# Five weight loads of an MM-DiT attention block issued as two transfers each

## The chip, the cores and the metric

The kernel runs on one core of one Trainium2 chip. The metric is the device time of one execution in microseconds (us). The time before is the median of three executions. Two numbers are kept apart: the device time, and the span of a profiled execution, which runs from the first instruction that the profiler records to the last one.

## The reference

Two streams of tokens, image (2 x 256 tokens) and text (2 x 32), share one attention. D is 1152, all tensors are bf16, and there is one head of width D.

```python
mod_i = (_silu(c) @ wmod_img).reshape(B, 6, 1, D)      # the same for _txt
shi, sci, gai = mod_i[:, 0], mod_i[:, 1], mod_i[:, 2]
hi = _layernorm(x_img) * (1 + sci) + shi               # ht from x_txt
qkvi = hi @ wqkv_img                                   # qkvt = ht @ wqkv_txt
q = concat([qt, qi]); k = concat([kt, ki]); v = concat([vt, vi])
p = softmax(einsum('bqd,bkd->bqk', q, k) * D ** (-0.5))
a = einsum('bqk,bkd->bqd', p, v)
out_i = x_img + gai * (a[:, Nt:] @ wo_img)
out_t = x_txt + gat * (a[:, :Nt] @ wo_txt)
```

Of the six modulation blocks of each `wmod` only the first three are read. So the core reads fourteen weight blocks of 1152 x 1152 (2592 KB each), seven per stream: shift, scale, gate, q, k, v and output.

## The kernel before

The contraction dimension is cut into KT = 9 rows of 128 partitions. A weight block lies in SBUF as a tile of 128 partitions x 9 x 1152, and every matmul that contracts over D runs a loop `kt` from 0 to 8 over that tile.

**Loads.** All weight loads go through the queue of SyncE (SP). The helper `load_w` (L73 to L77) takes one of the five buffers of the pool `w`, or a buffer that another tensor has left (argument `home`), and issues one `dma_start` at L76 for each pair in `ksplits`. `K3` cuts a block into three transfers of three rows (864 KB each), and `K2`, which is defined and used by no call, into one of five rows (1440 KB) and one of four (1152 KB). Without `ksplits` a block is one transfer of nine rows.

The loads that the change touches stand together at L443 to L453, in the order in which SP issues them: `w_k_i` (three parts), `w_sh_t`, `w_sc_t`, the text tokens `x_t` (144 KB), `w_q_t`, `w_k_t`, `w_ga_i`, `w_v_t` (three parts), `w_o_i`, `w_ga_t`, `w_o_t` (three parts). A load whose buffer is still being read waits on SP for the reader, and everything behind it on SP waits too.

**Who reads them.** The order of work is written out by hand (`manual_schedule`). TensorE runs, in this order: the image products (v at L255, q and k at L514); inside the k product the strips of the text modulation (`w_sh_t`, `w_sc_t` at L400 and L404) and the text q (`w_q_t`, L580); then the text k (`w_k_t`, L580); the scores with the image gate (`w_ga_i`, L630, L635 and L651); the text v (`w_v_t`, L688); the attention output (L753); the output projection of the image (`w_o_i`, L845), in its midst the text gate (`w_ga_t`, L818) and the text projection (`w_o_t`, L863); and the last chunks of the image. GpSimd (POOL) reads `w_o_i` once more at L829, to fold the gate into the last columns of the last chunk.

**Stores.** Image tiles 0 to 2 are stored whole at L856 from SP. The text output leaves in four pieces at L877, one from SP and three from ScalarE (ACT). The last image tile leaves in four pieces at L854: 384 and 384 columns from SP, 256 from ACT, and the last 128 from SP.

**Semaphores.** The framework gives each transfer that SP or ACT issues one of eight semaphores, in turn, called here H0 to H7. SP and ACT share the eight. Before a transfer is issued, its queue waits until the transfer eight places earlier, which had the same semaphore, has landed (where that is not yet known from an earlier wait). There are 51 such transfers, numbered here 0 to 50: 45 from SP and 6 from ACT. Number 50, the last store, thus has H2. The two stores before it, numbers 48 and 49, have H0 and H1. POOL's transfers have eight semaphores of their own.

**The end.** When the kernel's body is done (the profile gives this code the line L918), SP runs nine semaphore instructions: the first waits for two of POOL's semaphores, and the other eight for H0, H1, and so on to H7, each together with one semaphore of another engine or of POOL's queue. Then it drains, and two barriers over all engines follow.

Of the kernel before, what the change touches and what calls it, by code (L numbers as in the profile page):

```python
# [14 lines left out]
def kernel(  # L15
# [19 lines left out]
    B, NI, D = x_img.shape  # L35
# [34 lines left out]
    def w_view(src):  # L70
        return src.rearrange("(kt p) n -> p kt n", p=P)

    def load_w(src, c0, ksplits=((0, KT),), home=None):  # L73
        t = wpool.tile([P, KT, D], bf, tag="w", name="t") if home is None else act.tile([P, KT, D], bf, tag=home, name="w_home")
        for (k0, k1) in ksplits:
            nc.sync.dma_start(t[:, k0:k1, :], w_view(src)[:, k0:k1, c0:c0 + D])  # L76
        return t  # L77
# [36 lines left out]
    K2 = ((0, 5), (5, KT))  # L114
# [327 lines left out]

    w_k_i = load_w(wqkv_img, D, K3)  # L443
    w_sh_t = load_w(wmod_txt, 0)
    w_sc_t = load_w(wmod_txt, D)
    nc.sync.dma_start(x_t[0:P:P // NTT, :], xt_flat[:, :])
    w_q_t = load_w(wqkv_txt, 0)
    w_k_t = load_w(wqkv_txt, D)
    w_ga_i = load_w(wmod_img, 2 * D, home="V")
    w_v_t = load_w(wqkv_txt, 2 * D, K3)  # L450
    w_o_i = load_w(wo_img, 0)
    w_ga_t = load_w(wmod_txt, 2 * D)
    w_o_t = load_w(wo_txt, 0, K3)  # L453

# [468 lines left out]
```

## Time and profile before

| what | value |
|---|---|
| device time, three executions | 115.46, 115.46 and 115.82 us; median 115.46 us |
| device time of the profiled execution | 116.14 us |
| span of the profiled execution | 114.2 us (1.94 us of the device time lie around it) |
| granted TensorE clock | 1.00 |
| bytes read from HBM | 39.36 MB |
| last DVE instruction of the body | 111.19 to 111.48 us |
| last store (L854, SP) | issued at 111.52, landed 1.5 us later |

The span is counted from the first instruction that was recorded. PE is TensorE's matmul part, PEld its weight loading; a matmul's recorded length overlaps its successors', so that the distance between starts tells the pace. SP and the other sequencers show their transfers (the recorded length is the time that the queue took to issue one) and their semaphore instructions; what they waited for lies before the recorded start. A transfer's landing is the time at which its semaphore was full.

### The profile page before, as it was taken

Reading aid. Unit: us, or ns where it says so; the run is one execution under the profiler, and the core shown is the slowest. Engines: PE = TensorE matmul, PEld = TensorE weight load, DVE = VectorE, ACT = ScalarE, POOL = GpSimd, SP = SyncE. Lnnn points to the kernel's source line nnn. Section 1 sums busy time; section 2 is a strip of 40 time slices with the busy share of each in tenths; the row PEclk is TensorE's granted clock in tenths of the full one; section 3 lists DMA queues with packets and bytes.
Section 4 is the critical chain, followed back from the end, with each engine's and each line's share of the span. In section 5 each row is a group of like instructions: output and inputs, shape, how many; then the busy total and the mean of one; then the engine's idle time right before and its main releaser. Section 6 shows DMA issues by size and latency. Waiting matters only on the chain.

```text
span 114.2 us, 2916 instructions
## 1 busy us (share of the span) xinstructions
PE 108.5 (95%) x1227; PEld 64.9 (57%) x1227; DVE 76.1 (67%) x152; ACT 37.8 (33%) x87; POOL 27.5 (24%) x60
## 2 busy tenths in 40 slices
PE   5959999999999999999999999999999999999990
PEld 1336655655644444444447658787687565667660
DVE  1689430856199999999999860237666803998770
ACT  4618410272290062640008934015646700001000
POOL 7000111640050000000000050701550560799300
PEclk9999999999999999999999999999999999999999
DMA  3999999999999999999999999999999999963042
GB/s 77 346 377 343 373 379 403 412 410 411 404 412 411 407 418 399 411 412 411 412 412 412 411 404 408 404 400 395 411 409 405 407 413 398 384 248 109 22 168 69
DMA packets 22759, 40.87 MB, mean 358 GB/s; under 512 B 1295, under 2 KB 6555, under 8 KB 22747
## 3 DMA queue, kind: packets, MB, share of 16 engines
q1 hardware_dynamic: 21467, 39.05, 89.2%
q10 hardware_dynamic: 672, 0.77, 2.2%
q0 software_dynamic: 608, 0.88, 2.1%
q8 instruction: 9, 0.15, 0.5%
q14 instruction: 3, 0.02, 0.1%
HBM read 39.36 MB, written 1.34 MB: 356 GB/s over the span
## 4 chain that ended last, share of the span: by engine, by line
PE 90%; DMA 4%; DVE 2%; ACTq 0%; issue 0%
PE qkps L514 31%; PE ps L845 16%; PE va L255 14%; PE aps L753 5%; DMA x_i<-in_x_img_dram 4%; PE ps L580 4%; PE sps L613 4%; PE gps L400 3%; PE ops L863 2%; PE van L267 2%; PE ps L688 2%; PE mps L217 1%; DVE stats L166 1%; PE gps L818 1%; PE tp L208 1%; PE sps L626 1%
## 5 line engine op out<-in xcount | busy, mean ns | idle before, releaser
L514 PE MATMUL qkps<-hT_i,t 128*128 128x512 bf16 x162 | 35.6, 379 | 0.0
L514 PEld LDWEIGHTS <-t 128*128 128x128 bf16 x162 | 15.6, 98 | 18.6 <-issue 0.4
L476 DVE SCALAR_TENSOR_TENSOR sacc<-w_v_i,mod_img,sacc 128x1152 f32<-128x1152 bf16 x16 | 22.7, 1419 | 0.5
L255 PE MATMUL va<-w_v_i,hT_i 128*128 128x512 bf16 x72 | 17.5, 379 | 0.0
L845 PE MATMUL ps<-t,aT 128*128 128x384 bf16 x99 | 16.4, 326 | 0.0
L845 PEld LDWEIGHTS <-aT 128*128 128x128 bf16 x117 | 11.0, 98 | 6.8 <-issue 0.5
L851 DVE TENSOR_TENSOR tmp<-ps,gb 128x384 bf16<-128x384 f32 x11 | 6.1, 550 | 6.0 <-DMA gb<-mod_scratch 4.9
L829 POOL TENSOR_TENSOR w_og<-t,gb 128x384 bf16<-128x384 bf16 x9 | 8.6, 995 | 4.7 <-PE ps L845 4.7
L255 PEld LDWEIGHTS <-hT_i 128*128 128x128 bf16 x72 | 6.3, 97 | 5.7 <-ACT hT_i L201 0.2
L535 POOL TENSOR_SCALAR svn<-svr 128x128 bf16<-128x128 bf16 x1 | 0.3, 300 | 33.0 <-ACT svr L154 33.0
L166 DVE BATCH_NORM_STATS2 stats<-x_i 128x6 f32<-128x384 bf16 x12 | 5.9, 547 | 3.2 <-DMA x_i<-in_x_img_dram 3.2
L464 ACT ACTIVATE qT<-qkps 128x512 bf16<-128x512 f32 x9 | 4.7, 601 | 6.9 <-PE qkps L514 6.9
L480 ACT CAST shi<-sacc 128x1152 bf16<-128x1152 f32 x2 | 2.3, 1152 | 13.2 <-DVE sacc L476 13.2
L140 PE MATMUL wps<-wz 128*128 128x512 bf16 x15 | 5.5, 531 | 1.2 <-DVE wz L125 1.2
L240 POOL TENSOR_SCALAR hT_i<-hT_i,mod_img 128x128 bf16<-128x128 bf16 (+1 forms) x5 | 2.1, 438 | 15.7 <-ACT hT_i L201 9.3
L766 DVE TENSOR_SCALAR aT<-aps,sv 128x288 bf16<-128x288 f32 (+2 forms) x11 | 4.3, 456 | 1.9 <-PE aps L753 1.9
L235 DVE TENSOR_SCALAR hT_i<-hT_i,mod_img 128x256 bf16<-128x256 bf16 (+1 forms) x16 | 4.3, 328 | 1.7 <-ACT hT_i L212 1.6
L580 PEld LDWEIGHTS <-t 128*128 128x128 bf16 x162 | 4.9, 98 | 0.6 <-issue 0.4
L154 DVE CAST kT<-qkps 128x512 bf16<-128x512 f32 x3 | 2.1, 687 | 4.6 <-PE qkps L514 4.6
L580 PE MATMUL ps<-hT_t,t 128*128 128x64 bf16 x162 | 5.0, 193 | 0.0
L852 DVE TENSOR_TENSOR o<-tmp,x_i 128x384 bf16<-128x384 bf16 x11 | 4.8, 436 | 0.4
L768 ACT ACTIVATE aT<-aps,sv 128x288 bf16<-128x288 f32 (+2 forms) x11 | 4.0, 467 | 2.2 <-PE aps L753 2.2
(171 smaller groups left out, 147.4 us busy)
## 6 DMA issues: line engine op xcount, KB each, us to landing
t<-in_wmod_txt_dram SPq DMA_DIRECT2D x3, 2592.0 KB, 22.0
t<-in_wqkv_img_dram SPq DMA_DIRECT2D x6, 864.0 KB, 13.6
t<-in_wqkv_txt_dram SPq DMA_DIRECT2D x2, 2592.0 KB, 16.6
t<-in_wmod_img_dram SPq DMA_DIRECT2D x3, 864.0 KB, 11.7
w_home<-in_wmod_img_dram SPq DMA_DIRECT2D x1, 2592.0 KB, 13.6
t<-in_wqkv_txt_dram SPq DMA_DIRECT2D x3, 864.0 KB, 13.7
t<-in_wo_img_dram SPq DMA_DIRECT2D x1, 2592.0 KB, 18.0
t<-in_wo_txt_dram SPq DMA_DIRECT2D x3, 864.0 KB, 15.7
```

The source lines that it names most:

```text
L140: nc.tensor.matmul(ps[:], lhsT=wz[:, 0:P], rhs=wz[:], start=True, stop=True)
L166: nc.vector.bn_stats(stats[0:np_, k, :], x_ap[:, k * CH:(k + 1) * CH])
L255: nc.tensor.matmul(ps[:], lhsT=hT_i[:, kt, i * P:(i + 1) * P], rhs=w_v_i[:, kt, half * VW:(half + 1) * VW], start=(kt == 0), stop=(kt == K ...
L464: nc.scalar.mul(out_ap, in_ap, SCALE)
L476: nc.vector.scalar_tensor_tensor(saccs[b][:], w_v_i[:, kt, :], ap, saccs[b][:], op0=ALU.mult, op1=ALU.add)
L514: nc.tensor.matmul(pss[j - j0][:], lhsT=wq[:, kt, j * P:(j + 1) * P], rhs=hT_i[:, kt, :], start=(kt == 0), stop=(kt == KT - 1))
L580: nc.tensor.matmul(ps[:, j - j0, :], lhsT=wq[:, kt, j * P:(j + 1) * P], rhs=hT_t[:, kt, :], start=(kt == 0), stop=(kt == KT - 1))
L753: nc.tensor.matmul(bank[:, off:off + c1 - c0], lhsT=lhsT, rhs=rhs, start=(first[id(bank)] == n), stop=(final[id(bank)] == n))
L829: nc.gpsimd.tensor_mul(w_og[:, dt, 0:CH], w_o_i[:, dt, NG0:D], gb[:, B - 1, NG0:D])
L845: nc.tensor.matmul(ps[:, 0:cw], lhsT=aT[:, dt, t0:t0 + P], rhs=rhs, start=(dt == DTS[0]), stop=(dt == DTS[-1]))
L851: nc.vector.tensor_mul(tmp[:, 0:cw], ps[:, 0:cw], gb[:, b, cs])
L852: nc.vector.tensor_add(o[:, cs], tmp[:, 0:cw], x_i[:, i, cs])
```

## The change

Five of the loads get the argument `K2`, so that each is issued as a transfer of five rows and one of four. The order of the loads, their buffers, the bytes and the instructions of the compute engines stay as they are. The transfers of SP and ACT become 56, numbers 0 to 55, and all that come after the first added one move on in the round of eight semaphores. The last store is number 55 and has H7; the two before it have H5 and H6. Five matmuls or weight loads of PE, one multiplication of POOL and POOL's group of semaphore instructions ahead of L829 get a wait for the second part of a load.

```diff
     w_k_i = load_w(wqkv_img, D, K3)
     w_sh_t = load_w(wmod_txt, 0)
-    w_sc_t = load_w(wmod_txt, D)
+    w_sc_t = load_w(wmod_txt, D, K2)
     nc.sync.dma_start(x_t[0:P:P // NTT, :], xt_flat[:, :])
-    w_q_t = load_w(wqkv_txt, 0)
-    w_k_t = load_w(wqkv_txt, D)
-    w_ga_i = load_w(wmod_img, 2 * D, home="V")
+    w_q_t = load_w(wqkv_txt, 0, K2)
+    w_k_t = load_w(wqkv_txt, D, K2)
+    w_ga_i = load_w(wmod_img, 2 * D, K2, home="V")
     w_v_t = load_w(wqkv_txt, 2 * D, K3)
-    w_o_i = load_w(wo_img, 0)
+    w_o_i = load_w(wo_img, 0, K2)
     w_ga_t = load_w(wmod_txt, 2 * D)
     w_o_t = load_w(wo_txt, 0, K3)
```

The pairs that `ksplits` takes:

```python
    K3 = ((0, 3), (3, 6), (6, KT))
    K2 = ((0, 5), (5, KT))
```

## The prediction

> **What bounds the kernel now.** I first read the page's head and its chain of work that ended last.
>
> ```profile
> span 114.2 us, 2916 instructions
> GB/s 77 346 377 343 373 379 403 412 410 411 404 412 411 407 418 399 411 412 411 412 412 412 411 404 408 404 400 395 411 409 405 407 413 398 384 248 109 22 168 69
> PE 90%; DMA 4%; DVE 2%; ACTq 0%; issue 0%
> PE qkps L514 31%; PE ps L845 16%; PE va L255 14%; PE aps L753 5%; DMA x_i<-in_x_img_dram 4%; PE ps L580 4%; PE sps L613 4%; PE gps L400 3%; PE ops L863 2%; PE van L267 2%; PE ps L688 2%; PE mps L217 1%; DVE stats L166 1%; PE gps L818 1%; PE tp L208 1%; PE sps L626 1%
> ```
>
> The chain runs over TensorE for 90% of the span. The loads run at some 400 to 418 GB/s through most of it (a slice is 2.86 us), but DMA's 4% of the chain is the x tile at the start, and no other transfer is in it: PE does not wait for a weight. A change to the loads can therefore act in three places only: it makes a load late, it puts something into PE's own stream, or it acts behind the chain's end. The chain in order of time, from its middle and its end (start, length, what):
>
> ```profile
> 31.89 29.23 PE qkps L514 x135
> ...
> 66.48 1.94 PE qkps L514 x9
> ...
> 102.97 2.21 PE ops L863 x72
> 105.18 5.99 PE ps L845 x45
> 111.17 0.02 issue
> 111.19 0.29 DVE o L848
> ```
>
> It ends at 111.48, and the span at 114.2: 2.7 us lie behind the last arithmetic. The answers for line L918 on SP, asked in three windows, show what is there:
>
> ```profile
> L918 SPq EVENT_SEMAPHORE  x3: 28/28/28, 111.9 to 112.7; - x3
> ...
> L918 SPq EVENT_SEMAPHORE  x6: 28/28/28, 113.0 to 113.3; - x6
> ...
> L918 SPq DRAIN  x3: 7/7/13, 113.4 to 113.7; - x3
> ```
>
> These are the nine semaphore instructions and the drain. The first, for POOL's transfers, is at 111.9. H0 follows at 112.3 and H1 at 112.7, each when its store has landed, and H2 at 112.99 (the last store was issued at 111.52 and lands 1.5 later). H3 to H7 belong to transfers that landed long before, yet SP still runs one instruction for each: narrowing the window puts their starts at 113.05, 113.11, 113.17, 113.23 and 113.29, and the drain at 113.36. So a wait that is already satisfied costs SP (113.36 - 113.05) / 5 = 0.06 us, and five of them stand between the last landing and the barrier, on the path that sets the end.
>
> **The change, part by part.**
>
> *The end.* The last store moves from H2 to H7. SP issues it, as now, until 111.85, then passes POOL's semaphores and H0 to H4, whose transfers have all landed, in 6 x 0.06 = 0.36 us from 111.89, which is 112.25. H5, H6 and H7, which the last three stores now have, then pass as these land (112.3, 112.7, 112.99) and the drain follows 0.06 later, at 113.05 instead of 113.36. Removed: 5 x 0.06 = 0.30 us. The bounds are 5 x 28 ns (an instruction's own recorded length) = 0.14, and 0.37, the whole distance from 112.99 to the drain. I take 0.30, since it is the pace of the very instructions that move off the path. What waits for SP there is the barrier of all engines, which goes on from 113.4; nothing else ends so late.
>
> *The stream of loads.* Five transfers more, no byte more. The question is whether a cut leaves a gap. The rows below are two of the 864 KB parts and two whole loads of 2592 KB, with the time from issue to landing, and the last part of the last load:
>
> ```profile
> L76 SPq DMA_DIRECT2D t<-in_wqkv_img_dram x1: 2015/2015/2015, 21.2 to 21.2; - x1
> DMA to landing us min/median/max: 13.5/13.5/13.5
> ...
> L76 SPq DMA_DIRECT2D t<-in_wqkv_img_dram x1: 2020/2020/2020, 25.3 to 25.3; - x1
> DMA to landing us min/median/max: 13.7/13.7/13.7
> ...
> L76 SPq DMA_DIRECT2D t<-in_wqkv_txt_dram x1: 524/524/524, 45.3 to 45.3; - x1
> DMA to landing us min/median/max: 15.5/15.5/15.5
> ...
> L76 SPq DMA_DIRECT2D w_home<-in_wmod_img_dram x1: 367/367/367, 60.1 to 60.1; - x1
> DMA to landing us min/median/max: 13.6/13.6/13.6
> ...
> L76 SPq DMA_DIRECT2D t<-in_wo_txt_dram x1: 2036/2036/2036, 86.6 to 86.6; - x1
> DMA to landing us min/median/max: 15.6/15.6/15.6
> ```
>
> The first two parts land at 34.7 and 39.0 with one part between them: 2.15 us each. The two whole loads land at 60.8 and 73.7 with one whole load between them: 6.45 each, which is 3 x 2.15. So a cut costs nothing that these rows resolve: within 0.05 us, either way. Five cuts cost at most 5 x 0.05 = 0.25 us of delay at the stream's end, and the slack covers it. The tightest loads are the last parts of `w_o_t` and `w_v_t`. The former lands at 86.6 + 15.6 = 102.2, and its first reader, the 25th of 72 matmuls of L863, starts at 102.8 + 24 x 0.031 = 103.5 (L863's starts run from 102.8; 2.21 us / 72 = 0.031): 1.3 us. The latter lands at 67.0 + 13.8 = 80.8 and is first read at 82.3 (the 25th of 36 of L688): 1.5 us. If the cover were gone, the text projection would be late, then L872's chain to the text stores, and PE with it.
>
> *SP's queue.* Five issues more. An issue here takes 0.4 to 7 us, but that is SP waiting for room in a full queue, not work. `x_t` and everything later stand behind the added issues. The last load is issued by 88.6, and SP then waits 10.3 us, its longest wait in the answer on SP's waits, for the first store's data: that is the cover. Each added issue brings the wait for the transfer eight places back. The closest is `w_ga_t`, issued at 71.3, which would wait for the second part of `w_k_t`, landed by 67.2 (49.5 + 17.7): 4.1 us to spare.
>
> *PE's stream.* Five instructions get a wait for a second part that landed long ago (the closest is `w_o_i`, landed at 87.3, read from 89.9). A satisfied wait on a matmul seems free: matmuls 13 and 25 of L688 have one now, and start 0.206 us after their predecessors, like those without (0.205 to 0.208). From the chain's rows: 9 matmuls of L514 without such waits take 1.94, so 135 would take 29.1; the row has 29.23 with the waits for four later parts in it, at most 0.03 each, 0.16 for five. The far bound is a semaphore instruction of its own on PE's queue, 51 ns in the rows of L580: 5 x 51 = 0.26 us. I take 0, because the spacing of single matmuls is the nearest row.
>
> *POOL.* One more semaphore instruction (17 ns in POOL's rows of L918) and one attached wait ahead of and within L829. Its nine products run from 97.88 to 106.52 and are read from 109.5: 3 us of cover.
>
> The sum is -0.30 + 0 + 0 + 0 = -0.30 us. Against the profiled execution's own 116.14 (114.2 of span, 1.94 around it) that gives 115.84. The profiled execution is 0.68 above the median; the term should not depend on that, so the prediction is 115.46 - 0.30 = **115.16 us**, 0.26% less.
>
> **The rivals.**
>
> *A: the gain is eaten on PE.* If each new wait costs PE its 51 ns, 0.26 us return on the path and the time is 115.46 - 0.30 + 0.26 = 115.42, no change. For it: PE has no slack. Against: the equal spacing above, and that the built program has no more separate semaphore instructions on PE than before. The same end, 115.46, comes about if something else held the barrier to 113.4, or the semaphores went round otherwise than I counted; no engine's last instruction of the body but SP's lies near.
>
> *B: slower, the cuts open gaps in the stream.* The place is SP's transfers from `w_sc_t` on; it decides from a gap of 1.3 / 5 = 0.26 us per cut. The far row is the last store, a transfer with nothing queued around it: its 32 KB take 1.5 us from issue to landing, of which 0.08 are bytes at 410 GB/s. If a cut cost those 1.4 us, the last part of `w_o_t` would come 7.0 late, 5.7 beyond its slack: 115.16 + 5.7 = 120.9. Against it stand the equal paces above, with several transfers always queued.
>
> The Trainium skill speaks for B (DMA: Bandwidth & Descriptors, section Anatomy of one DMA): each transfer costs a fixed 2.0 us or so beside its bytes, by a fit for transfers that GpSimd issues. Five in series would be an estimated 10 us, 8.7 beyond the slack, and 123.9. The landings that this trace shows in SP's queue contradict it for queued transfers.
>
> *C: a larger gain.* A satisfied wait is dearer outside the profiled execution than in it. The distance from the last landing to the drain, 0.37 us, is the nearest row for more than 0.30: 115.09. Against it: recording an instruction should make it no cheaper.
>
> The Trainium skill (Advanced Engine Details and Errata, section Network/Comms) gives 50 to 100 ns for a sequencer's reading of a semaphore; at its upper end the five would be an estimated 0.5 us and the time 114.96, while this trace has 60 ns.
>
> **How the numbers follow.** About 0.3% of 115.46, 0.35 us, is what a measurement of this kernel can tell from no change, and the three runs spread over 0.36. My forecast has 0.82, A 0.10, B 0.05, C 0.03. The forecast's 0.30 lies just inside 0.35, so the scatter of a median, some 0.15, splits it nearly in half: 0.41 faster, 0.40 the same, 0.01 slower; its own range is 114.95 to 115.40. A gives 0.08 same and 0.02 slower, B 0.05 slower, C 0.03 faster. Together faster 0.44, same 0.48, slower 0.08. The range of 114.90 to 115.60 holds the forecast, A and C with their scatter, and leaves B out.
>
> **What would show it.** In the changed profile SP's first six semaphore instructions of L918 should stand close together from 111.9, three should follow at the landings, and the drain should start 0.06 after the last of them, not 0.37. The chain should still be PE with no new transfer in it, L580's two groups of 81 should keep 2.4 us each, and `w_o_t`'s last part should land at 102.2 within 0.3. A drain that keeps its distance from the last landing, a longer PE group at L400, L580, L630 or L845, or a load that lands past 103 would make it wrong.

## The result and the profile after

The changed kernel takes 115.07 us (median of 15 runs), the kernel before beside it 115.63 (15 runs). The ratio is 0.9956, with a 95% interval of 0.9940 to 0.9971, so 0.51 us less, between 0.34 and 0.69; one of the changed kernel's runs, 118.33 us at a granted clock of 0.984, was slow and is left out of the ratio. Run again on another occasion it took 115.08 against 115.49: ratio 0.9965 (0.9951 to 0.9979), 0.40 us less. The prediction was 0.30.

The profiled execution after took 115.07 us, and its span is 113.3. The page's head and chain:

```profile
span 113.3 us, 2923 instructions
PE 91%; DMA 6%; SPq 0%; DVE 0%; issue 0%
```

DMA's share is one load, as before, but another one: `w_sc_i` with 6.35 us at the start, where the x tile stood with 4.97. Both lie ahead of 31 us, where the two programs are the same. The chain in order of time from L514 on (start, length, what), the same pieces as before:

```profile
31.24 29.23 PE qkps L514 x135
...
65.83 1.94 PE qkps L514 x9
...
102.32 2.21 PE ops L863 x72
104.52 5.99 PE ps L845 x45
110.52 0.02 issue
110.54 0.29 DVE o L848
```

Apart from 0.02 us that two small neighbours (L496, L499) exchange, every piece from there on has the length that it had before. From the start of L514 to the end of the last DVE instruction there are 110.83 - 31.24 = 79.59 us, before 111.48 - 31.89 = 79.59. So nothing was gained or lost in the middle, where all the cuts and the new waits are. The profiled span is 0.9 shorter, and 0.65 of that lies ahead of 31 us, where the two programs are the same. This first phase varies from run to run: in the profile of the same changed kernel run again, L514 starts at 31.6. The profiled execution of before was a long one (116.14) and the one after an ordinary one (115.07), so their difference must not be read as the change's worth.

The loads, by the rows of L76 (time to issue, and from issue to landing), here the two parts of `w_q_t` and the last of `w_o_t`:

```profile
L76 SPq DMA_DIRECT2D t<-in_wqkv_txt_dram x1: 518/518/518, 45.2 to 45.2; - x1
DMA to landing us min/median/max: 12.7/12.7/12.7
...
L76 SPq DMA_DIRECT2D t<-in_wqkv_txt_dram x1: 2787/2787/2787, 45.8 to 45.8; - x1
DMA to landing us min/median/max: 15.0/15.0/15.0
...
L76 SPq DMA_DIRECT2D t<-in_wo_txt_dram x1: 2118/2118/2118, 86.7 to 86.7; - x1
DMA to landing us min/median/max: 15.4/15.4/15.4
```

The second part of `w_q_t` lands at 45.8 + 15.0 = 60.8, when the whole load landed before, and the last part of `w_o_t` at 102.1 (before 102.2). In this profile five more cuts left no gap in the stream. In that of the same kernel run again the last part lands at 102.96, so profiles of one kernel differ by more than the 0.25 us that the prediction allowed for five cuts.

The end, by the answers for L918 on SP in three windows:

```profile
L918 SPq EVENT_SEMAPHORE  x6: 27/28/28, 111.2 to 111.6; - x6
...
L918 SPq EVENT_SEMAPHORE  x3: 28/28/28, 111.6 to 112.3; - x3
...
L918 SPq DRAIN  x3: 7/7/13, 112.4 to 113.1; - x3
L918 SPq EVENT_SEMAPHORE  x2: 17/17/17, 113.0 to 113.2; - x2
```

Six satisfied waits run close together from 111.2, the last three pass at their stores' landings, and the drain starts at 112.42, 0.07 after the last wait and 0.09 after the last landing (112.33). Before it was 0.37 and 0.39. This is the predicted picture. But asked for what follows the second drain, the same view shows something new:

```profile
L918 SPq DRAIN  x1: 7/7/7, 112.5 to 112.5; - x1
...
nothing on L918; most used: []
...
L918 SPq EVENT_SEMAPHORE  x2: 17/17/17, 113.0 to 113.2; - x2
L918 SPq DRAIN  x1: 7/7/7, 113.1 to 113.1; - x1
```

From 112.49 to 112.98 SP does nothing (the middle view is of 112.50 to 112.95). Between the second drain and the next semaphore instruction there are 0.50 us (before 0.16), between the third drain and the last instruction 0.15 (before 0.46). From the first drain to the span's end it is 0.87 us instead of 0.84. So the end of the span gives a gain of 0.24 (2.47 us from the last DVE instruction to the span's end, before 2.70). The rest of the gain lies outside the span. The means over runs made side by side, each of which has its own span, say the same: 113.32 us of span and 1.80 around it for the changed kernel run again, 113.59 and 1.92 for the kernel before. Of the 0.38 between these sums 0.11 is in the time around the span, which the prediction had taken as fixed.

### The profile page after: what moved, and what is told of

Its sections match the earlier page's. It is cut to its first block, busy times and chain, and to the rows that moved or that the text cites. A ratio compares the mean times of both kernels' runs of the same rounds, so it can differ in the third digit from the quotient of the medians.

```text
span 113.3 us, 2923 instructions
## 1 busy us (share of the span) xinstructions
PE 107.9 (95%) x1227; PEld 64.5 (57%) x1227; DVE 75.7 (67%) x152; ACT 37.8 (33%) x87; POOL 27.5 (24%) x60
## 4 chain that ended last, share of the span: by engine, by line
PE 91%; DMA 6%; SPq 0%; DVE 0%; issue 0%
PE qkps L514 31%; PE ps L845 16%; PE va L255 14%; DMA w_sc_i<-in_wmod_img_dram 6%; PE aps L753 5%; PE ps L580 4%; PE sps L613 4%; PE gps L400 3%; PE mps L217 2%; PE ops L863 2%; PE van L267 2%; PE ps L688 2%; PE gps L818 1%; PE tp L208 1%; PE sps L626 1%; PE pk L697 1%
## 5 line engine op out<-in xcount | busy, mean ns | idle before, releaser
L514 PE MATMUL qkps<-hT_i,t 128*128 128x512 bf16 x162 | 35.6, 379 | 0.0
L514 PEld LDWEIGHTS <-t 128*128 128x128 bf16 x162 | 15.6, 98 | 18.6 <-issue 0.4
L829 POOL TENSOR_TENSOR w_og<-t,gb 128x384 bf16<-128x384 bf16 x9 | 8.7, 1001 | 4.4 <-DMA gb<-mod_scratch 4.4
L140 PE MATMUL wps<-wz 128*128 128x512 bf16 x15 | 5.0, 490 | 1.2 <-DVE wz L125 1.2
```

The source lines that it names most:

```text
L140: nc.tensor.matmul(ps[:], lhsT=wz[:, 0:P], rhs=wz[:], start=True, stop=True)
L514: nc.tensor.matmul(pss[j - j0][:], lhsT=wq[:, kt, j * P:(j + 1) * P], rhs=hT_i[:, kt, :], start=(kt == 0), stop=(kt == KT - 1))
L829: nc.gpsimd.tensor_mul(w_og[:, dt, 0:CH], w_o_i[:, dt, NG0:D], gb[:, B - 1, NG0:D])
```

## The experiments

Two sets of four kernels ran, each set on one chip beside the kernel before. In the first the number of transfers was varied.

**again56.** The changed kernel, unaltered.

> The changed kernel once more, as the base for the runs beside it. Theory E (only the end of SP's round of semaphores): 0.30 us below the kernel before, drain 0.06 to 0.09 us after the last store's landing. Theory L (the smaller loads also help somewhere ahead of the end): about 0.5 below, and the last DVE instruction ends earlier too, by about 0.2 on the mean of runs.

115.08 us, 0.40 below the kernel before (0.24 to 0.57). Its profile has 79.66 us from the first matmul of L514 to the end of the last DVE instruction by the instructions' own times, as have before and after (79.66 each): nothing is earlier ahead of the end except the first phase's scatter. Theory L's mechanism is not there, although its number is close.

**h0_57.** One cut more.

```diff
-    w_ga_t = load_w(wmod_txt, 2 * D)
+    w_ga_t = load_w(wmod_txt, 2 * D, K2)
```

> w_ga_t in two parts too: 57 transfers, the last store has H0, and seven satisfied waits stand behind its landing. Theory E: the drain 8 x 0.06 = 0.48 us after the last landing, the time 0.42 above the changed kernel, so 0.12 above the kernel before. Theory L: one more cut keeps or raises its 0.2, so the time is 0.1 below the kernel before or lower. If the end counts for nothing: as the changed kernel.

116.16 us, ratio 1.0054 (1.0035 to 1.0073): 0.62 above the kernel before and 1.08 above the changed one. One cut more undoes the gain, as theory E says, and then does more harm than the 0.42 that it allows. The answers for L918 show both:

```profile
L918 SPq EVENT_SEMAPHORE  x8: 27/28/28, 112.5 to 113.0; - x8
...
nothing on L918; most used: []
...
L918 SPq DRAIN  x2: 13/62/111, 113.0 to 113.5; - x2
```

H0 to H7 pass in eight steps from the last landing at 112.48, and the first drain is at 113.04, 0.56 after it (expected 0.48). Then SP stands still from 113.06 to 113.5, between the two drains. The kernel before has 0.06 there.

**h2_59.** Three cuts more than the changed kernel, which bring the last store back to H2.

```diff
-    w_k_i = load_w(wqkv_img, D, K3)
-    w_sh_t = load_w(wmod_txt, 0)
+    w_k_i = load_w(wqkv_img, D, ((0, 3), (3, 6), (6, 8), (8, KT)))
+    w_sh_t = load_w(wmod_txt, 0, K2)
...
-    w_ga_t = load_w(wmod_txt, 2 * D)
+    w_ga_t = load_w(wmod_txt, 2 * D, K2)
```

> w_ga_t and w_sh_t in two parts and w_k_i in four: 59 transfers, the last store has H2 as in the kernel before. Theory E: the drain 0.37 us after the last landing and the time that of the kernel before within 0.15. Theory L: 0.2 or more below the kernel before, for the cuts alone.

115.82 us, ratio 1.0038 (1.0017 to 1.0060): 0.44 above the kernel before. Both theories missed. Theory L's gain from cuts is refuted. Theory E lacks 0.4 us, and the profile shows where:

```profile
L918 SPq EVENT_SEMAPHORE  x5: 27/28/28, 112.4 to 112.7; - x5
...
nothing on L918; most used: []
...
L918 SPq DRAIN  x2: 7/20/32, 113.3 to 113.3; - x2
L918 SPq EVENT_SEMAPHORE  x1: 28/28/28, 113.2 to 113.2; - x1
```

The same standstill of nearly half a microsecond, here ahead of the wait for H7, with nothing to wait for.

**h7_48.** No load is cut; two are cut less, so that the last store is number 47 and has H7 (edit against the kernel before).

```diff
-    w_k_i = load_w(wqkv_img, D, K3)
+    w_k_i = load_w(wqkv_img, D)
...
-    w_o_t = load_w(wo_txt, 0, K3)
+    w_o_t = load_w(wo_txt, 0, K2)
```

> Nothing is cut: the five loads are whole as in the kernel before, w_k_i becomes one transfer and w_o_t two instead of three each: 48 transfers, the last store has H7. Theory E: drain 0.06 to 0.09 us after the last landing, 0.30 below the kernel before. Theory L: the end's 0.30 at most, and 0.2 more than the changed kernel.

115.29 us, ratio 0.9980 (0.9964 to 0.9997): 0.23 below the kernel before (0.03 to 0.42). Its drain is 0.08 after the last landing, and its span falls as expected (mean 113.28, 0.31 less than that of the kernel before beside it). The gain needs no cut; it comes with the place of the last store's semaphore. But the time around the span is 2.05, where the kernel before has 1.92.

**What the first set left open, and a new theory.** SP's program had 84 instructions in the changed kernel, 85 in h0_57 and 87 in h2_59. These are counts of the built program; the profile records two fewer in each kernel. Counted from the start, the standstill comes ahead of the 82nd instruction in all three (the 80th recorded). The kernel before (78) and h7_48 (75) end sooner, and their profiles show none. Theory F: SP stops for 0.47 us ahead of its 82nd instruction, and what it costs depends on where that instruction falls: nothing if SP would wait there anyway, 0.47 if it is on the path, and a part if the span is over by then. The second set tells this apart from the number of transfers, the semaphores and the cuts.

**sp85.** The changed kernel with one more text store on SP.

```diff
-        eng = nc.sync if g == 0 else nc.scalar
+        eng = nc.sync if g < 2 else nc.scalar
```

> The changed kernel with one text store (the second of four, L877) issued by SP instead of ACT. Still 56 transfers, the last store on H7, but SP's program has 85 instructions instead of 84. Theory F (SP stops for 0.47 us ahead of the 82nd instruction of its program, wherever that falls, as the profiles at 84, 85 and 87 instructions show): the gap falls between the two drains of L918, uncovered; span and time 0.48 above the changed kernel, so 115.56. Theory E (the round of semaphores alone): as the changed kernel, 115.08. If the stop belongs to the semaphore H0 or to the 57th transfer: as the changed kernel too.

115.66 us, ratio 1.0010 to the kernel before (0.9997 to 1.0023), so 0.58 above the changed kernel; expected was 115.56. Transfers, cuts and semaphores are the changed kernel's, and the whole gain is gone. Of the 0.58, 0.47 is in the end by the profiles (2.94 us from the last DVE instruction to the span's end, 2.47 in the changed kernel). This profile has a second loss, which has nothing to do with the stop: its chain runs over a load, the last part of `w_v_t`.

```profile
66.82 14.76 DMA t<-in_wqkv_txt_dram
81.58 0.04 issue
81.62 0.83 PE ps L688 x12
```

The 25th matmul of L688, its first reader, starts 0.43 us after its predecessor instead of 0.21, and the middle is 0.23 longer (79.89 against 79.66). How many of the other runs have this wait is not known. L918 on SP:

```profile
L918 SPq EVENT_SEMAPHORE  x1: 28/28/28, 112.4 to 112.4; - x1
L918 SPq DRAIN  x1: 13/13/13, 112.4 to 112.4; - x1
...
nothing on L918; most used: []
...
L918 SPq DRAIN  x2: 7/60/112, 112.9 to 113.3; - x2
L918 SPq EVENT_SEMAPHORE  x2: 17/17/17, 113.2 to 113.7; - x2
```

The drain follows the last wait by 0.07, then comes the stop between the drains (112.45 to 112.91). The view of this kernel's transfers from 112.0 to 113.8, in 40 slices, holds a single packet:

```profile
GB/s 0 0 0 0 0 0 0 0 0 0 0 0 0 0 0 0 0 0 0 0 0 0 0 0 0 0 0 0 0 0 0 0 0 0 182 0 0 0 0 0
DMA packets 1, 0.01 MB, mean 5 GB/s; under 512 B 0, under 2 KB 0, under 8 KB 0
...
q14 instruction: 1, 0.01, 1.2%
```

A transfer of instructions, 8 KB on queue 14, at 113.57 (slice 35), 0.66 after the stop's end. The profiles of after, again56, h0_57, h2_59 and h7_64 have the like 0.62 to 0.67 after the stop's end, and sp82 0.64 after the start of the 82nd instruction. In the kernel before it comes at 115.87, 1.7 us behind the span's end:

```profile
GB/s 0 0 0 0 0 0 0 0 0 0 0 0 0 0 0 0 0 0 0 0 0 0 0 0 0 0 0 0 0 131 0 0 0 0 0 0 0 0 0 0
DMA packets 1, 0.01 MB, mean 3 GB/s; under 512 B 0, under 2 KB 0, under 8 KB 0
...
q14 instruction: 1, 0.01, 1.3%
```

(The window here is 114.0 to 116.5.) This fits a stop in the kernel before too, in what SP runs behind the recorded span. It is not shown: no instruction is recorded there. In before_sp81 below, with three more instructions on SP, the packet comes 1.06 us behind the span's end, which fits as well.

**h7_64.** Thirteen transfers more than before instead of five.

```diff
-    w_sh_t = load_w(wmod_txt, 0)
-    w_sc_t = load_w(wmod_txt, D, K2)
+    w_sh_t = load_w(wmod_txt, 0, K3)
+    w_sc_t = load_w(wmod_txt, D, K3)
...
-    w_q_t = load_w(wqkv_txt, 0, K2)
-    w_k_t = load_w(wqkv_txt, D, K2)
-    w_ga_i = load_w(wmod_img, 2 * D, K2, home="V")
+    w_q_t = load_w(wqkv_txt, 0, K3)
+    w_k_t = load_w(wqkv_txt, D, K3)
+    w_ga_i = load_w(wmod_img, 2 * D, K3, home="V")
...
-    w_ga_t = load_w(wmod_txt, 2 * D)
+    w_ga_t = load_w(wmod_txt, 2 * D, K3)
```

> Every nine-row load of the list but w_o_i in three parts, w_o_i in two: 64 transfers, the last store again on H7, SP's program 92 instructions. Theory F: the gap falls among the satisfied waits ahead of the last stores' landings, where SP would wait anyway; drain 0.07 after the last landing; 115.04, the changed kernel's time or 0.04 less. Theory that each added transfer costs something, as 57 and 59 could also be read: 0.3 or more above the changed kernel.

115.04 us, ratio 0.9965 (0.9947 to 0.9982), as theory F had it. Its SP on L918:

```profile
L918 SPq EVENT_SEMAPHORE  x3: 28/28/28, 111.6 to 111.8; - x3
...
nothing on L918; most used: []
...
L918 SPq EVENT_SEMAPHORE  x5: 28/28/28, 112.2 to 112.5; - x5
```

The stop falls from 111.79 to 112.24, while the last store, which lands at 112.71, is still under way, and costs nothing. In time, thirteen cuts cost no more than five. But the last part of `w_o_t` lands at 103.20, the latest of the ten profiles and 0.04 ahead of its first reader, which starts 0.139 us after its predecessor instead of 0.112.

**sp82.** The changed kernel with all text stores on ACT.

```diff
-        eng = nc.sync if g == 0 else nc.scalar
+        eng = nc.scalar
```

> The changed kernel with all four text stores on ACT: 56 transfers, H7, SP's program 82 instructions. Theory F: the gap falls ahead of the very last semaphore instruction, where SP waits for the second barrier anyway; 115.05, as the changed kernel within 0.1. Theory that moving a text store between the queues matters by itself: a change of 0.3 or more.

115.09 us, ratio 0.9969 (0.9951 to 0.9987): the changed kernel's time. Moving a text store does nothing by itself.

**before_sp81.** The kernel before with all text stores on SP.

```diff
-        eng = nc.sync if g == 0 else nc.scalar
+        eng = nc.sync
```

> The kernel before with all four text stores on SP: 51 transfers, H2, SP's program 81 instructions instead of 78. Theory F: no gap inside the span, the span that of the kernel before (113.6 mean) and the time around it 1.80 instead of 1.92, because less of the stop is left for behind the span: 0.1 below the kernel before. If the move of stores costs: above it.

115.42 us, ratio 0.9992 (0.9978 to 1.0006). The median does not resolve the 0.1 us expected. The means go the way that was expected: span 113.62 (before 113.55), around it 1.80 (before 1.96). The drain is 0.38 after the last landing, as it should be with H2.

All of it in one table. "Behind" is the time from the last landing to SP's first drain, "end" the time from the last DVE instruction to the span's end (both from the one profile); "around" is the mean time outside the span over the kernel's runs.

| kernel | transfers, last store | SP instructions | behind | end | around | median |
|---|---|---|---|---|---|---|
| before | 51, H2 | 78 | 0.39 | 2.70 | 1.92 and 1.96 in two sets | 115.44 to 115.63 in three sets |
| changed | 56, H7 | 84 | 0.09 | 2.47 | 1.78 | 115.07 |
| again56 | 56, H7 | 84 | 0.09 | 2.46 | 1.80 | 115.08 |
| h0_57 | 57, H0 | 85 | 0.56 | 3.40 | 1.78 | 116.16 |
| h2_59 | 59, H2 | 87 | 0.88 with the stop | 3.23 | 1.79 | 115.82 |
| h7_48 | 48, H7 | 75 | 0.08 | 2.42 | 2.05 | 115.29 |
| sp85 | 56, H7 | 85 | 0.09 | 2.94 | 1.77 | 115.66 |
| h7_64 | 64, H7 | 92 | 0.08 | 2.43 | 1.80 | 115.04 |
| sp82 | 56, H7 | 82 | 0.08 | 2.41 | 1.78 | 115.09 |
| before_sp81 | 51, H2 | 81 | 0.38 | 2.72 | 1.80 | 115.42 |

The sum of "end" and "around" is 4.62 to 4.66 for the kernel before and 4.25 for the changed one, about 0.4 less. Taken off the median it leaves 110.8 to 111.0 us for every kernel of the table: what differs between them is in these two columns, but for the 0.2 us that are left. No kernel beats the changed one by more than the runs can tell.

## Why the prediction came out as it did

*The bound and the stages.* Right. The chain stayed PE's, from L514 on with the same lengths piece by piece.

*The end, -0.30 us.* Right in mechanism and size. The drain's distance to the last landing fell from 0.39 to 0.09. The cleanest pair is before_sp81 and sp82, in which no stop lengthens the end (in sp82 it falls where SP waits for the second barrier): 2.72 and 2.41 us from the last DVE instruction to the span's end, 0.31 apart. The six satisfied waits followed each other by 0.064 us where 0.06 was reckoned.

*The stream of loads, 0.* Right for the time, but the cover was over-sized. The prediction read 1.3 us of it in the profile whose first 31 us were the longest. Where PE gets through them sooner, the loads do not land sooner, and less cover is left between the last landing of `w_o_t` and its first reader: 0.77 us in the profile after, 0.35 in again56 (landed at 102.96, outside the 102.2 within 0.3 of the prediction's own test), 0.04 in h7_64, but also only 0.42 and 0.53 in h7_48 and before_sp81, where none of the five loads is cut. That PE waits for no weight held in the profiles of before and after; sp85's has such a wait of 0.23 us. So the 0 was right in the medians, with less room than was reckoned; whether each cut delays the stream a little is lost in the scatter between profiles. Rival B's 120.9 is far off the 115.07 measured. The Trainium skill (DMA: Bandwidth & Descriptors, section Anatomy of one DMA) gives a fixed 2.0 us per transfer, fitted to transfers that GpSimd issues. The estimate that takes it five times in a row, 123.9 us, is far off too: in SP's queue this cost did not add up while transfers were queued behind each other.

*PE's stream, 0, and POOL.* Right for the path. The stretch from the first matmul of L514 to the end of the last DVE instruction has all five new waits of PE in it and is 79.66 us in both profiles, which also settles rival A. POOL's products ended at 105.75 and were read from 108.85: 3 us of cover, as reckoned.

*SP's queue, covered.* Right for the loads (one issue, that of `x_t`, is longer than the 7 us given: 7.95 before, 2.70 after). What the step left out is that five more transfers also make SP's program longer, by six instructions.

*The step that failed* is the one from the span to the device time: "114.2 of span, 1.94 around it" was read as a constant. The time around the span fell by 0.11 us (1.92 to 1.80, side by side; the other sets' means give up to 0.19), and in the changed kernel SP's stop lies in the first barrier, where it costs the span some 0.05. That sum, -0.30 + 0.05 - 0.11 to -0.19, is -0.36 to -0.44 us and lies inside both intervals (0.34 to 0.69 and 0.24 to 0.57), while -0.30 is inside the second and just outside the first. That both have one cause, a stop that before was paid behind the span, fits but is argued. The gain was thus 0.1 to 0.2 larger than predicted; that the predicted time still came within 0.09 of 115.07 is in part luck, since the base of three executions, 115.46, lies 0.17 below the 115.63 beside the result. The time came nearest to rival C's 115.09, but nothing points to C's mechanism: the mean span of the runs fell by 0.27, and the end in the profiles by 0.24.

*Same or faster.* The chances were split by scatter about 0.30. The extra 0.1 to 0.2, for which only C had a price (0.37 us in all, at a chance of 0.03), put both medians beyond the 0.35 us.

*A narrow escape.* One more instruction on SP, as in sp85, would have left no gain at all, and the prediction had no case for that.

## What to carry to other kernels

Where a queue waits for a round of semaphores in a fixed order at the end, count the transfers: the last one to land should hold the semaphore that is waited for last, and each satisfied wait behind it costs 0.06 us here. Count the instructions of the queue that ends the kernel too, since a stop at a fixed place in its program can eat a gain of this size; its place is seen by asking the profile for a stretch in which that queue shows nothing although nothing holds it. And before two profiled spans are compared, compare a stretch in which the programs are equal: here the first 31 us alone differed by 0.65. The cover of a load is read from several profiles for the same reason: here it was 1.3 us in the profile of before, 0.53 in that of before_sp81 with the same loads, and 0.77 and 0.35 in two of the changed kernel.

## What the runs showed of the hardware

SP stopped for 0.44 to 0.49 us ahead of the 82nd instruction of its program in every kernel in which this could be seen as a gap in its own stream (84, 85, 87 and 92 instructions), and an 8 KB transfer of instructions on queue 14 started 0.62 to 0.67 us after the stop's end. That the stop is SP crossing from one block of its instructions to the next fits both, but was not shown by itself: no run changed the block or its place. The Trainium skill (Runtime: NRT & Kernel Launch, section Instruction fetch mechanics) says that a sequencer fetches its instructions in blocks by its own DMA queue, and that crossing a block's border is mostly hidden. Here the stop was hidden in h7_64, where SP would have waited for a store anyway. Where SP itself ended the kernel, it made the end 0.53 us longer: 3.23 in h2_59 against 2.70 before, both with the last store on H2, and 2.94 in sp85 against 2.41 in sp82, both with H7.

Two things stay open: why the time around the span is 2.05 us for a program of 75 instructions, 1.92 to 1.96 for 78 and 1.77 to 1.80 from 81 on, which fits a stop that is paid in part behind the span, and what makes the first 31 us vary by 0.9 from profile to profile (L514's first matmul starts between 30.96 and 31.83 us in the ten profiles).
